# Two VectorE operations of the first division moved one period later, in a fused routing-attention and act-serf kernel

## The chip, the cores and the metric

The kernel runs on one core of a Trainium2 chip. The metric is the device time of one execution, in microseconds; the time of a kernel is the median over its runs. The engines named below are TensorE (PE in the profile, its weight loads PEld), VectorE (DVE), ScalarE (ACT), GpSimd (POOL) and SyncE (SP), which here only issues DMAs (SPq is its queue).

## What is computed

Attention for 4 batches, 8 heads, 768 positions and 64 values per head, where a query sees only the keys that fall to the same of 16 centroids; its output is the input of a two-layer network with a gate between the layers.

```python
q_assign = np.argmax(np.einsum('bhsd,hcd->bhsc', q_n, c_n), axis=-1)
k_assign = np.argmax(np.einsum('bhsd,hcd->bhsc', k_n, c_n), axis=-1)
mask = q_assign[:, :, :, None] == k_assign[:, :, None, :]
scores = scale * np.matmul(q, k.transpose(0, 1, 3, 2))
scores = np.where(mask, scores, -1000000000.0)
scores = scores - np.max(scores, axis=-1, keepdims=True)
attn = np.exp(scores)
attn = attn / (np.sum(attn, axis=-1, keepdims=True) + 1e-09)
attn_out = np.matmul(attn, v)
...
h = x @ w_in                                  # x: 3072 x 512, w_in: 512 x 2048
sp = np.maximum(h, 0.0) + np.log1p(np.exp(-np.abs(h)))
g = h * erf(sp)
out = g @ w_out                               # w_out: 2048 x 512
```

## The kernel before

The 32 heads are worked on in 16 pairs, numbered from 0. A pair has 12 units: a unit is one half of the queries (384 of 768) against one tile of 128 keys, six units to a half. The attention runs as a sequence of periods, `period(p, i)` with i from 0 to 5, and each period does the matmuls of two units, so six periods make a pair and three make a half. The second layer of the kernel, the network, follows and takes the rest of the span.

Every engine call goes through a wrapper that keeps the program's order on its engine, so what is written first in `period` runs first on that engine. No planner moves anything there; the queues are in the order in which the Python code makes them, and semaphores between engines follow from which tile is written and read.

A period has these parts, in the order of the code:

- A step of the maxima, `step_ahead(p, 2 * i)`. For a tile of 128 queries of a later half or pair, low-precision products go into the PSUM tile `wide` (rows `wide<-kv,qv`, then `wide<-km,qm`, which add the routing mask), and VectorE reduces them to the negated maxima, `nmx<-wide`. There is one `wide`, so the next step's matmuls wait for this reduction.
- A call of `next(part[0], None)`, which advances a division by one piece (below).
- The products of query and key of the first unit, `sc<-qT,kT`, then `mask(3)`, then those of the second unit. Where the table `FIRST_MASKS` (for the first pair) or `MASKS` (for the others) has an entry, `mask` issues a matmul `turned<-hotT,pick` or `turned<-aside,pick` that writes 384 columns of a PSUM tile `turned`, and ScalarE copies these to the mask rows `qm` or `km`. For the first pair the table has an entry at i = 5, place 3: the second half of `qm` of the second pair, in `turned[0]`.
- A second step of the maxima, `step_ahead(p, 2 * i + 1, True)`, in three pieces, with the mask matmuls of the scores, `sc<-qm,km`, between its matmuls. These need the row of shifts of their half (the negated row maxima), which is row 0 and row 64 of `qm`.
- The second call of `next(part[0], None)`, which is the one that the change touches (L1466).
- ScalarE's exponentials, `pr<-sc`, the sums over units on GpSimd, `more_out<-more_out,pr`, and the products with the values, `turned<-pr,in_v`, of the two units before.
- At i = 0 and i = 3 the start of the division of the half just finished.

A step that ends a half also calls `into_rows`: VectorE reduces the maxima to `least`, transposes them to `least_rows`, and SyncE issues four DMAs `qm<-least_rows` that put the row of shifts in place. In the first pair, i = 5, the first step (the tenth that is counted from the pair's start) does this for the first half of the second pair; `scores` of the second pair's first unit, in the period after, reads that row.

`divide(u)` is a generator. Its first piece issues the matmuls `turned<-more_out,minus` and two ScalarE operations `inv`. The second piece is VectorE's `den<-turned,inv` and the first `turned<-turned,inv` (128x192). The third is the second `turned<-turned,inv` and then `more_out<-den,turned` (128x384), which reads the numerators out of the PSUM tile `turned` and leaves the quotients in SBUF. The fourth issues four DMAs `x_dram<-more_out`. The first division (the first half of the first pair) begins at i = 3 and has its numerators in `turned[0]`. Its second and third piece come at i = 4, one at each call of `next(part[0], None)`, and its fourth at the first call in i = 5.

Of the kernel before, what the change touches and what calls it, by code (L numbers as in the profile page):

```python
# [28 lines left out]
HJ = NJ // 2  # L29
# [110 lines left out]
def kernel(  # L140
# [182 lines left out]
    def sign(n):  # L323
        hi, _, upper = steps[n]
        ae.activation(out=upper, in_=hi, func=ACT.Prelu, scale=2.0**-25, alpha=2.0**90)
# [51 lines left out]
    def transposes(p, which="qk"):  # L377

        if p >= NPAIR:
            return  # L380
        st = pairs[p]
        for nm in which:
            st[nm + "T"] = rows[p % 3][nm]
            ve.transpose(out=st[nm + "T"], in_=st.pop(nm).rearrange("p n t -> p (n t)"))
        if "k" in which:
            st.update(lows[p % 2])
            if p > 1:
                load_qk(p + 1)
# [10 lines left out]
    def similarities(p, groups=range(4), lo=0, hi=HW):  # L399

        if p >= NPAIR:
            return
        st = pairs[p]
        st["psim"] = turned[1][:, 0:HW]
        for g in groups:
            te.matmul(
                st["psim"][2 * C * g : 2 * C * (g + 1), lo:hi], lhsT=ccT[:, p % HP],
                rhs=st["qk"[g // 2] + "T"][:, g % 2 * HW + lo : g % 2 * HW + hi],
                start=True, stop=True,
            )  # L410

    def choose(p, spare=None, aside=False):

        if p >= NPAIR:
            return
        st = pairs[p]
        n = HW // C
        sims = routep.tile([P, HW], F32, name="sims")
        ve.transpose(out=sims, in_=st.pop("psim"))
        yield  # L420
        sim = sims.rearrange("p (g c) -> p g c", c=C)
        mx = (wide[:, 0] if spare is None else spare)[:, 512 - n :]
        ve.reduce_max(out=mx, in_=sim, axis=AX.X)
        yield
        hot = routep.tile([P, HW], BF16, name="hot")
        ve.tensor_tensor(
            out=hot.rearrange("p (g c) -> p g c", c=C), in0=sim,
            in1=mx.unsqueeze(2).to_broadcast([P, n, C]), op=ALU.is_equal,
        )
        yield  # L430
        if aside:
            st["aside"] = routep.tile([P, HW], BF16, name="aside")
            ve.transpose(out=st["aside"][D + Q :], in_=hot[D : D + Q])
            yield
        st["hotT"] = routep.tile([P, HW], BF16, name="hotT")
        ve.transpose(out=st["hotT"], in_=hot)
# [5 lines left out]
    def masks(p, nm, half, bank, narrow=False, copied_by=ae):  # L442

        if p >= NPAIR:
            return lambda: None
        st = pairs[p]
        cols = slice(half * HW, (half + 1) * HW)
        r, hot = slice(0, D) if nm == "q" else slice(D, P), st["hotT"]
        picked = pick[r, half]
        if narrow:  # L450
            r = slice(r.start + Q, r.stop)
            picked = pick[r, 1]
            hot = hot if half else st["aside"]
        won = bank[:, 0:HW]
        te.matmul(won, lhsT=picked, rhs=hot[r], start=True, stop=True)
        if nm == "q":
            return lambda: ae.activation(out=st["qm"][:, cols], in_=won, func=ACT.Relu)
        if copied_by is ve:
            return lambda: ve.tensor_scalar(
                out=st["km"][:, cols], in0=won, scalar1=BIG, scalar2=nbig, op0=ALU.mult, op1=ALU.add  # L460
            )
        return lambda: ae.activation(
            out=st["km"][:, cols], in_=won, func=ACT.Identity, bias=nbig, scale=BIG
        )
# [82 lines left out]
    def turn(p, h):  # L547

        st = pairs[p]
        pn = turned[h][:, 0:HW].rearrange("p (t n) -> p t n", t=HJ)  # L550
        for t in range(HJ):
            for e in range(2):
                cols = slice(e * D, e * D + Q)
                te.matmul(pn[cols, t], lhsT=lowest[h][:, t, cols], rhs=identb, start=True, stop=True)
        for e in range(2):
            r = slice(e * D, e * D + 1)
            ae.copy(out=st["qm"][r, h * HW : (h + 1) * HW], in_=pn[r].rearrange("p t n -> p (t n)"))
        st["shift", h] = True
# [832 lines left out]
    def run(work):  # L1391
        for _ in work:
            pass
# [19 lines left out]
    part = [iter(())]  # L1413

    def period(p, i):
        u = 2 * NJ * p + 2 * i
        n1, n2 = 2 * p - 1, 2 * p
        early = lambda n: 0 <= n < N_EARLY

        def mask(place):  # L1420
            which = (MASKS if p else FIRST_MASKS).get((i, place))
            if which:
                return masks(p + 1, *which, turned[0 if i in (0, 5) else 1], place == 2)
            return lambda: None

        if u > 0:
            for which in turns if i in (0, 3) else ():
                turn(*which)
                turns.remove(which)
            if i == 3 and not p:  # L1430
                transposes(2, "k")
            if i == 3 and p:
                similarities(p + 2)
                routing[0] = choose(p + 2, turned[0], True)
            step_ahead(p, 2 * i)
            if i == 3 and p:
                next(routing[0], None)
            if i == 2:
                transposes(p + 2, "k" if p else "q")
        mask(0)()  # L1440
        if i == 0 and early(n1 - 1):
            sign(n1 - 1)
        elif i == 3 and early(n1):
            sign(n1)
        if i == 4:
            next(routing[0], None)
        next(part[0], None)
        if i == 0 and p:
            run(routing[0])
            transposes(p + 2, "q")  # L1450
        if u == 2:
            next(routing[0])
            next(routing[0])
        products(u)
        mask(3)()
        products(u + 1)
        mask(1)()
        second = step_ahead(p, 2 * i + 1, True) if u > 0 else iter(())
        next(second, None)
        if u == 0:  # L1460
            step_ahead(0, 1)
        rows = D if u == 0 or u + NJ + 2 >= len(units) else Q
        scores(u, rows)
        next(second, None)
        next(second, None)
        next(part[0], None)  # L1466
        if i == 5:
            next(routing[0], None)
        scores(u + 1, rows)
        later = mask(2)  # L1470
        if i == 3 and not p:
            similarities(p + 2)
            routing[0] = choose(p + 2, turned[0], True)
        if i == 0:
            later()
            curve(u)
        else:
            curve(u)
            later()
        curve(u + 1)  # L1480
        if u == 0:
            similarities(1)
            routing[0] = choose(1, turned[1])
            next(routing[0])
            vectors(1, "q")
            vectors(1, "k")
        if i == 0 and early(n1 - 1):
            bounded(n1 - 1)
            shifted(n1 - 1)
        elif i == 1 and early(n1):  # L1490
            size_and_rest(n1)
        elif i == 5 and early(n2):
            rest(n2)
        for _ in range(FORMS.get(p, {}).get(i, 0)):
            x_forms.pop(0)() if x_forms else forms.pop(0)[0]()
        if i == 3:
            if not p:
                next(routing[0], None)
            if early(n1):
                bounded(n1)  # L1500
                shifted(n1)
        elif i == 1:
            load(p + 1, "v", v, vp)
            if p == 0:
                run(routing[0])
        elif i == 4:
            vectors(p + 2, "k")
            vectors(p + 2, "q")
        if u > 0:
            if i == 1 and early(n1 - 1):  # L1510
                summed(n1 - 1)
            elif i == 4 and early(n1):
                summed(n1)
            if i in POOL_FORMS.get(p, ()) and forms:
                forms.pop(0)[1]()
            for w in (u - 2, u - 1):
                accumulate(w)
            for w in (u - 2, u - 1):
                attend(w)
            if i == 3:  # L1520
                next(routing[0], None)
            if i % HJ == 0 and u - 1 != LATE or u - 3 == LATE:
                part[0] = divide(u - 1 - u % NJ)
                next(part[0])
        if i == 3 and early(n2):
            size(n2)
# [74 lines left out]
    u = len(units)  # L1601
# [101 lines left out]
```

## Time and profile before

| | us |
|---|---|
| median of 3 runs | 945.91 |
| lowest and highest of them | 945.71 and 1938.44 |
| the profiled execution | 945.83 |
| its span, first to last instruction | 944.1 |
| TensorE busy in the span | 938.0 |
| VectorE busy in the span | 784.3 |
| period i = 4 of the first pair, by its first `wide` matmul | from 33.45 |
| period i = 5 of the first pair | from 37.40 |
| period i = 0 of the second pair | from 41.49 |

The profiled execution took 1.73 us more than its span; that is what lies before the first and after the last instruction. In a timeline each row has the start and the duration in microseconds, the engine, the line, the operation, what it writes and reads, and how many instructions are merged in it; a bracket at the end gives the idle time before it and what ended that. All instructions carry L131, since the wrapper of the engines issues them, so they are told apart by their tiles. In the chain of waits each row is a stretch of the path that ended last.

### The profile page before, as it was taken

The page shows a single profiled execution, that of the slowest core. Times are in us where ns is not written, and L with a number is a line of the kernel's source. Part 1 is how long each engine was busy: PE and PEld are TensorE (multiplying, and loading weights), DVE is VectorE, ACT ScalarE, POOL GpSimd, SP SyncE. Part 2 cuts the span into 40 slices and gives each one's busy share as a digit, 9 for nine tenths or more (in the row PEclk, how much of TensorE's full clock was granted, in tenths as well). Part 3 has the DMA queues.
Part 4 walks back from the last instruction along what each step waited for, and adds up shares of the span by engine and source line. Part 5 has one row for each costly group of instructions (what it writes and reads, how often), then busy time and mean ns, then how long its engine had stood idle before and what let it go on. Part 6 is the DMA issues. An engine that isn't in the chain of part 4 may idle for free.

```text
span 944.1 us, 22367 instructions
## 1 busy us (share of the span) xinstructions
PE 938.0 (99%) x8775; PEld 708.9 (75%) x8775; DVE 784.3 (83%) x1416; ACT 546.6 (58%) x809; POOL 506.4 (54%) x365
## 2 busy tenths in 40 slices
PE   8999999999999999999999999999999999999998
PEld 4555555555555555688888889998999899989987
DVE  8888888888888887879886688689868977897887
ACT  4777777777777776476413553663257236525541
POOL 2688888888888888999119111450063016103600
PEclk9999999999999999999999999999999999999999
DMA  9345545554443621133875257353453436343433
GB/s 215 79 112 113 113 113 114 113 114 112 113 112 68 156 56 38 24 128 127 219 249 219 83 125 221 106 175 118 151 176 128 136 120 202 118 150 123 157 112 111
DMA packets 176352, 123.17 MB, mean 130 GB/s; under 512 B 132600, under 2 KB 143352, under 8 KB 176248
## 3 DMA queue, kind: packets, MB, share of 16 engines
q1 hardware_dynamic: 171880, 116.34, 43.2%
q0 software_dynamic: 1872, 4.98, 2.9%
q8 instruction: 69, 1.13, 0.5%
q10 hardware_dynamic: 2496, 0.43, 0.2%
q14 instruction: 35, 0.29, 0.1%
HBM read 91.78 MB, written 23.33 MB: 122 GB/s over the span
## 4 chain that ended last, share of the span: by engine, by line
PE 98%; DVE 1%; SPq 0%; DMA 0%; issue 0%; DVEq 0%
PE bank L131 43%; PE turned L131 32%; PE sc L131 17%; PE wide L131 6%; DVE nmx L131 1%; SPq L131 0%; DMA qm<-least_rows 0%; DVE sims L131 0%; DVE hotT L131 0%; DVE wide L131 0%; DVE hot L131 0%; DVE qm L131 0%; DVE qT L131 0%; DVE osb L131 0%; DVEq L1698 0%
## 5 line engine op out<-in xcount | busy, mean ns | idle before, releaser
L131 POOL TENSOR_TENSOR more_out<-more_out,pr 128x768 f32<-128x768 f32 x128 | 217.1, 1696 | 15.4 <-ACT pr L131 5.4
L131 DVE TENSOR_REDUCE nmx<-wide 128x2 f32<-128x512 f32 (+4 forms) x189 | 179.4, 950 | 45.6 <-PE wide L131 44.5
L131 ACT ACTIVATE pr<-sc 128x768 f32<-128x768 f32 x192 | 148.4, 810 | 80.4 <-PE wide L131 73.8
L131 PE MATMUL turned<-pr,in_v 128*32 128x193 f32 x3072 | 145.2, 330 | 0.0
L131 POOL TENSOR_TENSOR g<-g 128x512 f32<-128x512 f32 x36 | 47.1, 1308 | 180.8 <-DVE g L131 178.9
L131 PEld LDWEIGHTS turned<-pr,in_v 128*32 128x32 f32 x3072 | 90.2, 109 | 51.0 <-issue 27.0
L131 DVE TENSOR_TENSOR g<-g 128x512 f32<-128x512 f32 x132 | 90.8, 688 | 23.2 <-PE bank L131 12.2
L131 PE MATMUL sc<-qT,kT 64*128 64x384 f32 x528 | 98.7, 485 | 0.0
L131 DVE TENSOR_TENSOR g<-bank,g 128x256 f32<-128x256 f32 (+1 forms) x128 | 64.6, 531 | 18.2 <-PE bank L131 9.5
L131 PE MATMUL bank<-g_more,g 128*128 128x256 f32 (+1 forms) x328 | 75.7, 374 | 0.0
L131 PE MATMUL bank<-x_own,w_in 128*128 128x128 f32 (+1 forms) x440 | 74.0, 310 | 0.0
L131 ACT ACTIVATE a_s<-g 128x1024 f32<-128x1024 f32 x38 | 39.6, 1055 | 57.5 <-POOL g L131 44.7
L131 POOL TENSOR_TENSOR more_out<-pr,pr 128x768 f32<-128x768 f32 x32 | 59.6, 1861 | 14.9 <-ACT pr L131 14.9
L131 PEld LDWEIGHTS bank<-g_more,g 128*128 128x128 f32 x328 | 61.2, 190 | 8.1
L131 PEld LDWEIGHTS bank<-x_own,w_in 128*128 128x128 f32 x440 | 63.2, 191 | 4.4 <-issue 0.6
L131 DVE TENSOR_TENSOR g<-a_s,g 128x512 f32<-128x512 f32 x76 | 66.2, 892 | 0.4 <-ACT a_s L131 0.4
L131 PE MATMUL wide<-kv,qv 64*128 64x512 bf16 (+4 forms) x380 | 64.4, 326 | 0.5 <-DVE nmx L131 0.5
L131 PE MATMUL bank<-w_out,g 128*128 128x256 f32 x280 | 64.5, 379 | 0.0
L131 PE MATMUL wide<-km,qm 32*128 32x512 bf16 (+5 forms) x380 | 62.0, 325 | 0.0
L131 ACT ACT_TABLE_LOAD x40 | 51.3, 1283 | 17.9 <-DVE g L131 17.3
L131 PEld LDWEIGHTS <-qv 64*128 64x128 bf16 x386 | 23.0, 93 | 51.4 <-issue 37.1
L131 PEld LDWEIGHTS sc<-qT,kT 64*128 64x128 f32 x528 | 46.3, 187 | 18.6 <-issue 1.3
(245 smaller groups left out, 1992.6 us busy)
## 6 DMA issues: line engine op xcount, KB each, us to landing
g_more<-b_dram SPq DMA_DIRECT2D x52, 512.0 KB
g_more<-w_dram SPq DMA_DIRECT2D x84, 256.0 KB
x_own<-in_moe_w_in_dram SPq DMA_DIRECT2D x13, 512.0 KB
in_v<-in_v_dram SPq DMA_DIRECT2D x32, 192.0 KB
x_dram<-more_out SPq DMA_DIRECT2D x128, 48.0 KB
x_own<-x_dram SPq DMA_DIRECT2D x6, 1024.0 KB
in_k<-in_k_dram SPq DMA_DIRECT2D x59, 96.0 KB
in_q<-in_q_dram SPq DMA_DIRECT2D x58, 96.0 KB
```

The costliest lines, as they stand in the source:

```text
L131: ins = getattr(self.engine, name)(*args, **kw)
```

## The change

One call of `next(part[0], None)` is left out in one period, that of u = 8, which is the first pair at i = 4 (HJ is 3, and u is 12 p + 2 i).

```diff
@@ -1463,7 +1463,8 @@
         scores(u, rows)
         next(second, None)
         next(second, None)
-        next(part[0], None)
+        if u != 2 * (HJ + 1):
+            next(part[0], None)
         if i == 5:
             next(routing[0], None)
         scores(u + 1, rows)
```

The generator of the first division is thereby one piece behind at the end of i = 4. Its third piece comes at the first call in i = 5, which stands behind the first step of that period and its `into_rows`, and its fourth at the second call of i = 5. On VectorE the order was

```
nmx x2 | turned<-turned,inv | more_out<-den,turned | nmx | least | memset nmx | least_rows | nmx
```

and is now

```
nmx x2 | nmx | least | memset nmx | least_rows | turned<-turned,inv | more_out<-den,turned | nmx
```

No instruction is added or taken away, on this engine or another. On SyncE the four `x_dram` DMAs follow the four `qm<-least_rows` DMAs in both kernels. TensorE, ScalarE and GpSimd have the same instructions in the same order.

## The prediction

> **What bounds the kernel now.** I read the page's totals first, then the chain of waits from the period after the change to the end, then the same chain around the change.
>
> ```profile
> span 944.1 us, 22367 instructions
> PE 938.0 (99%) x8775; PEld 708.9 (75%) x8775; DVE 784.3 (83%) x1416; ACT 546.6 (58%) x809; POOL 506.4 (54%) x365
> by line: PE bank L131 45.2%; PE turned L131 32.2%; PE sc L131 16.6%; PE wide L131 5.7%; DVE osb L131 0.0%; DVEq L1698 0.0%; issue 0.0%
> ```
>
> The third line is the chain restricted to 44 us and later, that is, to everything behind the place of the change. Its four TensorE entries add up to 99.7%. TensorE's queue is the path from there to the end, so a delay of that queue, or a gain, near 40 us should reach the end in full. Now the chain at the change:
>
> ```profile
> 36.07 1.28 DVE L131 TENSOR_REDUCE nmx<-wide 128x2 f32<-128x352 f32 x2
> 37.26 0.42 DVE L131 SCALAR_TENSOR_TENSOR turned<-turned,inv 128x192 f32<-128x192 f32 x1
> 37.72 0.56 DVE L131 SCALAR_TENSOR_TENSOR more_out<-den,turned 128x384 f32<-128x384 f32 x1
> 38.19 1.05 DVE L131 TENSOR_REDUCE nmx<-wide 128x2 f32<-128x864 f32 x1
> 39.35 0.18 DVE L131 TENSOR_REDUCE least<-nmx 128x6 bf16<-128x18 f32 x1
> 39.58 0.27 DVE L131 STREAM_TRANSPOSE least_rows<-least 128x96 bf16<-128x96 bf16 x1
> 40.06 1.23 DVE L131 TENSOR_REDUCE nmx<-wide 128x2 f32<-128x1024 f32 x1 [0.20 <-PE wide L131]
> ```
> ```profile
> 40.00 0.75 SPq L131
> ...
> 41.93 1.49 DMA qm<-least_rows
> 43.42 0.14 issue
> 43.56 0.34 PE sc L131 x2
> ```
> ```profile
> 37.40 0.36 PE L131 MATMUL wide<-kv,qv 64*128 64x432 bf16 x2
> 37.58 0.36 PE L131 MATMUL wide<-km,qm 64*128 64x432 bf16 x2
> 37.76 0.82 PE L131 MATMUL sc<-qT,kT 64*128 64x384 f32 x4
> 38.40 0.32 PE L131 MATMUL turned<-hotT,pick 64*128 64x384 bf16 x1
> 38.42 0.95 PE L131 MATMUL sc<-qT,kT 64*128 64x384 f32 x4
> 39.30 0.39 PE L131 MATMUL wide<-kv,qv 64*128 64x512 bf16 x2
> 39.62 0.33 PE L131 MATMUL sc<-qm,km 32*128 32x384 bf16 x2
> 39.63 0.39 PE L131 MATMUL wide<-km,qm 32*128 32x512 bf16 x2
> 41.49 0.28 PE L131 MATMUL wide<-kv,qv 64*128 64x256 bf16 x2
> 43.56 0.34 PE L131 MATMUL sc<-qm,km 32*128 32x384 bf16 x2 [0.17 <-DMA qm<-least_rows]
> ```
>
> The first fence is VectorE: the two operations to be moved (37.26 and 37.72) and, right behind them, the row step that ends in `least_rows`. The second is the one stretch behind 20 us where the chain leaves TensorE for a transfer: the row of shifts, issued by SyncE from 40.00, lands at 43.42, and the second pair's first scores begin at 43.56 because of it. The third is TensorE over the same time. Two things matter in it: the scores at 43.56 wait, and the mask's matmul `turned<-hotT,pick` at 38.40 stands ahead of everything else of that period.
>
> **The moved operations, and what they hold up.** In the old order they take VectorE from 37.26 to 38.19, 0.93 us ahead of the row step. That step's matmuls end at 37.58 + 0.36 = 37.94, and a reduction starts 0.04 behind the matmuls it waits for (39.63 + 0.39 = 40.02 against 40.06). With the two gone from the front it starts at 37.98: the row gains 0.21 us and not 0.93, because TensorE is then the late one.
>
> The rest of the row step keeps its spacing: `least` 1.16 behind the reduction (38.19 to 39.35), `least_rows` 0.23 behind that (39.35 to 39.58), so 39.14 and 39.37. The memset between them has no room of its own in the old order and gets none here. What follows such a transpose without a wait starts 0.20 later, as in the second pair:
>
> ```profile
> 51.10 0.28 DVE L131 STREAM_TRANSPOSE least_rows<-least 128x96 bf16<-128x96 bf16 x1
> 51.30 0.95 DVE L131 STREAM_TRANSPOSE kT<-in_k 128x768 f32<-128x768 f32 x1
> ```
>
> The first moved operation therefore starts at 39.57, the second 0.46 later (37.26 to 37.72), at 40.03, and it ends 0.56 later, at 40.59. In the old order that end was 37.72 + 0.56 = 38.28.
>
> This end releases the mask's matmul. The matmul writes 384 columns of `turned[0]`; the second moved operation reads the first division's numerators from the same columns (386 of them), so the matmul may not start before it has ended. In the old order it began at 38.40, 0.12 behind that end, with the first unit's products just through, so the wait cost nothing visible. Now it begins about 0.05 behind 40.59 (the `wide` matmuls at 37.40 begin 0.05 behind the reductions that hold them, 36.07 + 1.28 = 37.35): at 40.64. **TensorE stands for 40.64 - 38.40 = 2.24 us.** Queued behind this matmul on TensorE are the second unit's products, the second step of the maxima, both units' mask scores and the products with the values; ScalarE's exponentials wait for the scores, GpSimd's sums for the exponentials, VectorE's next reduction for `wide`. Nobody has other work to offer TensorE there.
>
> What the stall consists of is thus VectorE's own chain: 1.05 + 0.18 + 0.27 of the row step with its gaps, which the mask never had to wait for, and the 0.93 of the moved pair, less the 0.21. I take the stall as between 2.1 and 2.4 us: the gaps between VectorE operations in these rows scatter by about 0.1, and so does the release.
>
> **What the stall pays back.** Two waits that TensorE has now lie behind it.
>
> ```profile
> 45.82 0.28 PE L131 MATMUL wide<-kv,qv 64*128 64x256 bf16 x2
> 47.65 0.34 PE L131 MATMUL sc<-qm,km 32*128 32x384 bf16 x2
> 50.41 0.96 PE L131 MATMUL sc<-qT,kT 64*128 64x384 f32 x4
> 51.47 0.34 PE L131 MATMUL sc<-qm,km 32*128 32x384 bf16 x2
> ```
>
> First, the transfer. From the first `wide` matmul of a period to its first mask scores takes 47.65 - 45.82 = 1.83 us where nothing is waited for, and 43.56 - 41.49 = 2.07 in the period that waits for the row. The wait is worth 0.24 us. In the new order the row lands 0.21 earlier, at 43.21, while TensorE arrives two microseconds later, so it is gone altogether. Second, the wait for `wide`. From the second unit's products to the mask scores takes 51.47 - 50.41 = 1.06 in a period with a mask at the same place, and 39.62 - 38.42 = 1.20 here, where the second step's matmuls at 39.30 follow the row step's reduction (38.19 + 1.05 = 39.24). By then the reduction is long done, so 0.14 goes. Together 0.38 us come back.
>
> The other queues: the `x_dram` DMAs stood behind the row's four DMAs on SyncE already.
>
> ```profile
> 42.48 1.82 SPq L131 DMA_DIRECT2D x_dram<-more_out  x4
> 38.76 0.50 ACT L131 ACTIVATE qm<-turned 128x384 bf16<-128x384 f32 x1
> 41.01 3.45 POOL L131 TENSOR_TENSOR more_out<-more_out,pr 128x768 f32<-128x768 f32 x2 [0.72 <-ACT pr L131]
> 45.38 0.51 PE L131 MATMUL turned<-more_out,minus 128*32 128x192 f32 x8
> ```
>
> Their source is ready at 40.59, before SyncE gets to them at 42.48 - 0.21 = 42.27; this costs nothing, and the cover, 1.7 us, is ample. ScalarE's copy of the mask begins 0.36 behind its matmul (38.40 to 38.76) and lasts 0.50; shifted it ends at 41.50. The `wide<-km,qm` matmuls that read it stand at 39.63 and come at 39.63 + 2.24 - 0.14 = 41.73, so 0.23 us of cover is left; if ScalarE were later than that, the rest would be added. GpSimd's sum ends at 41.01 + 3.45 = 44.46 and its reader on TensorE starts at 45.38: 0.92 us of slack, of which the vanished transfer wait eats 0.24. All of these move with TensorE, and none becomes the late one.
>
> **Sum.** 2.24 - 0.14 - 0.24 = +1.86 us on the profiled execution: 945.83 + 1.86 = 947.69. The median of the runs shown, 945.91, lies 0.08 higher, which is less than the spread of the runs that agree (945.71 to 945.91), so I state 947.7.
>
> **Rivals.**
>
> *The mask does not wait* (faster). The place is the matmul at 38.40. If it, or the products behind it, can run while VectorE is still busy with the row step, only the gains are left: the 0.14, and 0.21 of the 0.24, as the row lands 0.21 earlier. That is 945.83 - 0.35 = 945.48. It decides at 38.40: if the matmul still starts there, this holds. For it speaks that no row shows this matmul waiting; against it that its output columns and the ones that the division reads are the same, and that in the old order it started only 0.12 us behind the division's end. [...] Chance 0.05.
>
> *The stall is absorbed later* (no change, 945.83). This needs a place behind 44 us where TensorE waits for something that does not move with it. The restricted chain above leaves 0.3% for all else, so I see none. Chance 0.03.
>
> *ScalarE becomes late.* If the copy of the mask comes later than its 0.23 us of cover allows, at most its length of 0.50 is added: 948.2. Chance 0.08.
>
> *The stall costs TensorE its clock.*
>
> ```profile
> 0.00:4.00 4.00, 2.87 (x14) 1.87 (x15) 1.91 (x21) 1.69 (x3) 2.97 (x21) 1.00 0.67 107
> 40.00:44.00 4.00, 3.83 (x57) 1.98 (x53) 3.84 (x5) 3.44 (x4) 3.20 (x3) 1.00 0.08 19
> ```
>
> In these rows by stretches (bounds, length, busy time of PE, PEld, DVE, ACT and POOL, then the granted clock) the clock is 1.00, with 1.13 us of TensorE idle in the first and 0.17 in the second. No row has a gap of 2.24 us. If the clock were halved for one period after it, the work between 41.49 and 45.82 would take 4.33 us more: 947.69 + 4.33 = 952.0. [...] Chance 0.04.
>
> **How the numbers follow.** The forecast has 0.80; the chances of the five add up to 1. Its own bounds are 945.83 + 2.1 - 0.38 = 947.55 and 945.83 + 2.4 = 948.23, where nothing is paid back. With twice the runs' spread of 0.20 on either side this is 947.15 to 948.63, and I give 947.1 to 948.6. It takes in the late ScalarE and leaves out the mask that does not wait, the absorbed stall and the lost clock, 0.12. Two per cent, about what a measurement of this kernel can tell from no change, is 18.9 us; every case here stays far within it, so I give 0.98 to that and 0.01 to each side for what I have not thought of.
>
> **What would show it.** On VectorE, `least_rows` about 0.2 us earlier and `more_out<-den,turned` ending near 40.6. On TensorE, the mask's matmul near 40.6 with an idle time of about two microseconds before it that names VectorE, and scores in the next period without a wait for `qm<-least_rows`. In the chain, a stretch of VectorE between 38 and 40.6 in place of the transfer. The prediction is wrong if the mask's matmul still stands near 38.4, if the distance of TensorE's rows to those of the kernel before shrinks again after 50 us, or if the granted clock falls under 1.00.

## The result and the profile after

| | before | after |
|---|---|---|
| median, us | 945.85 (8 runs) | 949.20 (8 runs) |
| the profiled execution, us | 945.83 | 949.37 |
| its span, us | 944.1 | 947.7 |
| mean granted TensorE clock in it | 1.000 | 0.998 |

The ratio of the times is 1.0031, with a 95% interval from 1.0021 to 1.0040 (the two medians alone would give 1.0035). One of the eight runs of the kernel before took 1938.44 us and is left out of the ratio. The changed kernel is slower by a third of a per cent, and the 949.20 lies above the range of 947.1 to 948.6. The eight runs of the changed kernel fall on two levels: three at 947.49, 947.60 and 947.60 with a mean clock of 1.000, and five from 949.14 to 949.44 with a clock of 0.998. The profile is of one on the upper level.

The first fence is VectorE and the head of TensorE's waits, from the timeline and the list of waits of the changed kernel (a wait row has the total, the number of waits and the longest).

```profile
37.97 1.06 DVE L131 TENSOR_REDUCE nmx<-wide 128x2 f32<-128x864 f32 x1 [0.63 <-PE wide L131]
39.37 0.27 DVE L131 STREAM_TRANSPOSE least_rows<-least 128x96 bf16<-128x96 bf16 x1
39.57 0.40 DVE L131 SCALAR_TENSOR_TENSOR turned<-turned,inv 128x192 f32<-128x192 f32 x1
40.00 0.55 DVE L131 SCALAR_TENSOR_TENSOR more_out<-den,turned 128x384 f32<-128x384 f32 x1
PE turned L131 <- DVE more_out L131: 2.0, 1, 2.0
```

The row step starts 0.22 us earlier (37.97 for 38.19), waits for TensorE as foretold, and the moved pair ends at 40.55. The new wait of TensorE names `more_out`. Now TensorE's own timeline:

```profile
40.61 0.47 PE L131 MATMUL turned<-hotT,pick 64*128 64x384 bf16 x1 [2.03 <-DVE more_out L131]
40.62 1.74 PE L131 MATMUL sc<-qT,kT 64*128 64x384 f32 x4
42.06 0.73 PE L131 MATMUL wide<-kv,qv 64*128 64x512 bf16 x2
42.72 0.50 PE L131 MATMUL sc<-qm,km 32*128 32x384 bf16 x2
43.47 1.75 PE L131 MATMUL turned<-pr,in_v 128*32 128x193 f32 x32
45.15 0.28 PE L131 MATMUL wide<-kv,qv 64*128 64x256 bf16 x2
46.99 0.34 PE L131 MATMUL sc<-qm,km 32*128 32x384 bf16 x2
```

The mask's matmul starts at 40.61, with 2.03 us of idle time before it. The durations behind it have changed too. The four products behind it take 1.74, where the same four took 0.95 in the kernel before; the `wide` pair takes 0.73 in place of 0.39. From the mask's matmul to the next period's first `wide` matmul are 45.15 - 40.61 = 4.54 us, in the kernel before 41.49 - 38.40 = 3.09. From there the old pace is back: 46.99 - 45.15 = 1.84, with no wait for the row of shifts, which was 2.07 with it. The stretches of 0.4 us below (bounds, length, busy time of PE, PEld, DVE, ACT and POOL, and then the granted clock) tell why:

```profile
38.40:38.80 0.40, 0.18 (x2) 0.00 (x0) 0.40 (x1) 0.40 (x1) 0.32 (x2) 1.00 0.00 0
...
40.00:40.40 0.40, 0.00 (x0) 0.00 (x0) 0.40 (x1) 0.00 (x0) 0.30 (x1) 1.00 0.00 0
40.40:40.80 0.40, 0.19 (x2) 0.19 (x3) 0.16 (x1) 0.00 (x0) 0.00 (x0) 0.74 0.00 0
40.80:41.20 0.40, 0.40 (x3) 0.40 (x4) 0.00 (x0) 0.08 (x1) 0.00 (x0) 0.50 0.01 1
...
43.60:44.00 0.40, 0.40 (x8) 0.26 (x11) 0.40 (x1) 0.40 (x1) 0.00 (x0) 0.50 0.51 123
44.00:44.40 0.40, 0.40 (x17) 0.24 (x10) 0.40 (x1) 0.40 (x2) 0.12 (x1) 0.99 0.48 117
```

The granted clock is 0.50 in every stretch from 40.80 to 44.00. A mean of 0.74 in the stretch before means that it fell 0.21 us ahead of 40.80, at 40.59; a mean of 0.99 in the last one, that it rose at 44.01. It was halved for 3.42 us, and half of that, 1.71 us, is lost if all of TensorE's work runs at half its pace. The two levels differ by 949.3 - 947.6 = 1.7.

### The profile page after: what moved, and what is told of

Same layout as the page of the kernel before. It is cut to its first block, busy times and chain, and to the rows that moved or that the text cites. A ratio compares the mean times of both kernels' runs of the same rounds, so it can differ in the third digit from the quotient of the medians.

```text
span 947.7 us, 22368 instructions
## 1 busy us (share of the span) xinstructions
PE 939.6 (99%) x8775; PEld 709.3 (75%) x8775; DVE 783.3 (83%) x1416; ACT 546.5 (58%) x809; POOL 506.7 (53%) x365
## 4 chain that ended last, share of the span: by engine, by line
PE 98%; DVE 1%; issue 0%; DVEq 0%
PE bank L131 43%; PE turned L131 32%; PE sc L131 17%; PE wide L131 6%; DVE nmx L131 1%; DVE sims L131 0%; DVE hotT L131 0%; DVE wide L131 0%; DVE more_out L131 0%; DVE hot L131 0%; DVE qm L131 0%; DVE qT L131 0%; DVE turned L131 0%; DVE osb L131 0%; DVEq L1699 0%
```

## The experiments

The two theories before them: A, that the stall costs 1.7 us by itself, and that the idle time before the mask's matmul halves the clock in some runs, which costs another 1.7; B, that the second level has another cause and the clock only goes with it.

**The idle time filled with useless matmuls.** In the changed kernel, between the products of the first unit and the mask:

```diff
         products(u)
+        if u == 10:
+            filler = ps_s.tile([P, 2, 512], F32, name="sc", tag="s")
+            of_filler.append(filler)
+            for _ in range(FILL):
+                te.matmul(filler[:, 0, 0:P], lhsT=identb, rhs=identb, start=True, stop=True)
         mask(3)()
```

`FILL` is 18, a constant in a new line ahead of the wrapper, so that the rows of this kernel carry L132. In a line that is not shown, the second unit's products take `filler` as their tile and overwrite it.

> The changed kernel, with 18 matmuls 128x128 of no use put on TensorE between the first unit's products and the mask's matmul, into a PSUM tile that the second unit's products overwrite. They fill the time in which TensorE stood idle (2.03 us in the profile after) and should fit into it. Theory A (the stall costs 1.75 us, and in some runs TensorE's clock is halved after it because of the idle time, which costs another 1.7): the stall stays, the clock does not fall, all runs at 947.4 to 947.8 with a mean clock of 1.000. Theory B (the second level of the runs has another cause in the changed order, and the clock only marks it): still two levels, some runs near 949.3.

Measured: 947.70 against 945.82, ratio 1.0020 (1.0011 to 1.0029). All 11 runs lie from 947.43 to 947.98, three of them above the 947.8 that was expected, with a clock of 1.000. From TensorE's timeline of this kernel:

```profile
38.25 1.18 PE L132 MATMUL sc<-identb 128*128 128x128 bf16 x18
40.34 0.32 PE L132 MATMUL turned<-hotT,pick 64*128 64x384 bf16 x1 [0.91 <-DVE more_out L132]
40.35 0.95 PE L132 MATMUL sc<-qT,kT 64*128 64x384 f32 x4
41.45 0.34 PE L132 MATMUL sc<-qm,km 32*128 32x384 bf16 x2
43.33 0.28 PE L132 MATMUL wide<-kv,qv 64*128 64x256 bf16 x2
45.16 0.34 PE L132 MATMUL sc<-qm,km 32*128 32x384 bf16 x2
```

The mask still waits for the same VectorE operation and as long (2.85 us from the first unit's products to the mask here, from 37.49, and in the changed kernel, from 37.76), but only 0.91 us of it is idle, and the products behind it take 0.95 again. The upper level is gone, and the stall's own price is left. This separates the two parts: B is refuted. The useless matmuls change what TensorE did last as well as the length of its idle time; the experiment with three of them, below, separates these.

**The mask's matmul out of the way.** In the changed kernel the table's entry moves from i = 5 to i = 3, where it writes `turned[1]`:

```diff
-FIRST_MASKS = {(2, 0): ("q", 0), (2, 3): ("k", 0), (2, 2): ("k", 1), (5, 3): ("q", 1)}
+FIRST_MASKS = {(2, 0): ("q", 0), (2, 3): ("k", 0), (2, 2): ("k", 1), (3, 1): ("q", 1)}
```

> The changed kernel, with the mask's matmul of i = 5 moved to i = 3, where it writes the other PSUM tile and has nothing to do with the first division. The new order on VectorE stays. Theory A: the whole loss is this matmul's wait, so nothing of it is left: 945.7 to 945.9, clock 1.000, no TensorE wait for more_out<-den,turned. Rival (the two operations cost time where they now stand, because VectorE gets behind): 946.5 or more.

Measured: 945.90 against 945.82, ratio 1.0002 (0.9993 to 1.0010). The whole loss hung on this one matmul. Two rows of this kernel show that the new order is not free, though, only paid for elsewhere:

```profile
40.49 1.22 DVE L131 TENSOR_REDUCE nmx<-wide 128x2 f32<-128x1024 f32 x1
41.76 0.28 PE L131 MATMUL wide<-kv,qv 64*128 64x256 bf16 x2 [0.39 <-DVE nmx L131]
```

With TensorE no longer standing, VectorE's next reduction is the late one (behind the moved pair, without idle time), and `wide` comes free 0.39 us late.

**The same move in the old order.** The table's entry as above, in the kernel before.

> The kernel before, with only the mask's matmul moved from i = 5 to i = 3; the order on VectorE is the old one. It tells what that move is worth by itself. If the new order costs nothing once the mask is out of the way and gains nothing either (the run with both was 945.90), this is 945.8 to 945.95. If the new order did bring the row's 0.2 us there and something else ate it, this run shows a wait for qm<-least_rows near 0.2 us and no wait of wide for nmx at 41.76.

Measured: 945.99 against 945.79, ratio 1.0002 (0.9993 to 1.0011), a little above what was expected. The wait for the row of shifts is there (0.16 us of idle time before the scores at 43.69), that of `wide` for `nmx` is not. So the new order did buy off the row's wait, for one of about the same size. By the first `wide` matmuls of the periods, i = 5 takes 4.35 us with the new order (37.41 to 41.76) and 4.10 with the old (37.53 to 41.63), and the period after it 4.10 (to 45.86) and 4.32 (to 45.95).

**One more reduction ahead of the moved pair.** The idle time becomes longer:

```diff
+        if u == 10:
+            idle_for = small.tile([P, 1], F32, name="idle_for")
+            ve.reduce_max(out=idle_for, in_=rows_of_first["q"], axis=AX.X)
         next(part[0], None)
```

> The changed kernel, with one more VectorE reduction (128x768, near 0.95 us, of no use) ahead of the two moved operations, so that TensorE stands idle for about 3.0 us in place of 2.0. [...] Theory B: the same mixture as before, some runs near 948.5 and some near 950.2.

Measured: five runs, at 948.22 (clock 1.000), 949.69, 949.69, 949.77 (0.997 to 0.998) and 951.17 (0.996), against 945.82, ratio 1.0041 (1.0028 to 1.0054). TensorE stood idle for 2.88 us. Four of five fell (here and below, a run has fallen when its mean clock is 0.998 or less). My levels were 0.3 to 0.5 too high: the idle time grew by 0.85 us and not by 0.95, and the levels lie 1.5 apart and not 1.7; the rest is open. The run at 951.17 lost about twice as much clock as the others. The mask's matmul and the clock in the profile of the run at 949.77:

```profile
41.23 0.32 PE L131 MATMUL turned<-hotT,pick 64*128 64x384 bf16 x1 [2.88 <-DVE more_out L131]
```
```profile
41.20:41.60 0.40, 0.36 (x3) 0.35 (x4) 0.00 (x0) 0.01 (x1) 0.00 (x0) 1.00 0.01 1
...
42.00:42.40 0.40, 0.40 (x4) 0.00 (x0) 0.00 (x0) 0.08 (x1) 0.00 (x0) 0.75 0.01 1
42.40:42.80 0.40, 0.40 (x8) 0.13 (x6) 0.00 (x0) 0.00 (x0) 0.00 (x0) 0.50 0.01 1
...
45.20:45.60 0.40, 0.40 (x12) 0.12 (x4) 0.00 (x0) 0.40 (x1) 0.40 (x1) 0.50 0.00 0
45.60:46.00 0.40, 0.40 (x12) 0.20 (x6) 0.00 (x0) 0.40 (x1) 0.32 (x2) 0.98 0.00 0
```

Here TensorE is at work again from 41.23 on at the full clock, and the clock falls only at 42.20, 0.97 us later, and rises at 45.62: once more 3.42 us. In the profile of the changed kernel it fell at 40.59, 0.02 us ahead of the mask's matmul. The idle time began at 41.23 - 2.88 = 38.35 here and at 37.76 + 0.82 = 38.58 there, so the fall comes 3.85 and 2.01 us behind its beginning. It is thus at no fixed distance from the idle time's end or its beginning; what places it, these two profiles do not show.

**The pair between the reduction and `least`.** A shorter idle time:

```diff
             else:
+                if (p, h) == (1, 0):
+                    next(division[0])
                 into_rows(p, h, nmx, HJ - 1 if in_parts else 0, HJ)
```

In a line that is not shown, `division` is made another name of `part`, the list with the generator.

> The two moved operations stand behind the row step's reduction, but ahead of least and least_rows. TensorE stands idle for about 1.4 us in place of 2.0 and loses 1.57 against the old order, of which 0.14 and 0.24 come back. [...] Theory B: two levels, 947.0 and 948.7, in a mixture like that of the changed kernel.

Measured: 946.88 against 945.82, ratio 1.0010 (1.0001 to 1.0019). Idle for 1.43 us, all 11 runs between 946.67 and 947.01, none fell.

**One of the two moved.** In the kernel before, the first division gets one more stop, so that only `more_out<-den,turned` comes behind the row step:

```diff
-            if k == 0:
+            if k == 0 or u == NJ - 1:
                 yield
```

> Only the second of the two operations, more_out<-den,turned, is moved behind the row step; the first keeps its old place, and the mask stays at i = 5. TensorE then stands idle for about 1.6 us. The stall is 0.43 shorter than in the changed kernel: 947.1 (946.95 to 947.3). [...] Rival (any long gap can cool it, the chance growing smoothly with the gap): some runs near 948.7.

Measured: 947.17 against 945.79, ratio 1.0015 (1.0006 to 1.0024). Idle for 1.56 us, none of 11 runs fell.

**Three useless matmuls.** The first experiment with `FILL = 3`:

> The changed kernel with 3 matmuls of no use in the gap in place of 18, which leaves TensorE idle for about 1.85 us. [...] Rival (what the 18 matmuls changed was not the length of the gap but what TensorE had just done): one level at 947.6.

Measured: seven runs, median 947.78 against 945.79, ratio 1.0027 (1.0016 to 1.0038). Idle for 1.75 us. That is 0.10 less than expected. Two runs fell (949.32 and 949.86, clock 0.998), so that useless matmuls alone do not keep the clock. Four lie from 947.45 to 947.78; one at 948.32, with a clock of 1.000, fits neither level and I can't explain it.

**Two more reductions.** The experiment with a longer idle time, with its reduction twice:

> [...]

Measured: six runs, median 951.67 against 945.86, ratio 1.0063 (1.0050 to 1.0075). Idle for 3.86 us. All six fell, three with a clock of 0.998 (950.94 to 951.16) and three with 0.996 (952.17 to 952.46). Half of the runs thus lost about twice as much clock, and their times lie 1.0 to 1.5 us above the others. The profile of the run at 951.16, in stretches of 1 us:

```profile
40.00:41.00 1.00, 0.00 (x0) 0.00 (x0) 0.96 (x2) 0.00 (x0) 0.23 (x1) 1.00 0.00 0
...
43.00:44.00 1.00, 1.00 (x11) 0.12 (x6) 0.00 (x0) 0.22 (x1) 0.00 (x0) 0.77 0.41 98
...
46.00:47.00 1.00, 1.00 (x18) 0.27 (x12) 0.00 (x0) 0.97 (x2) 0.92 (x2) 0.52 0.00 0
```

TensorE is idle from 38.52 to 42.38. The clock falls at 43.54, 1.16 us after TensorE is at work again, and rises at 46.96: 3.42 us once more.

**The changed kernel again.**

> The changed kernel itself, to see the two levels on the same chip as the longer gap. [...] Rival (the share of cooled runs belongs to the chip or the day): another share, near none or near all.

Measured: all five runs fell, from 949.19 to 949.60, against 945.86. With the eight above that is 10 of 13. Five of five is also what the rival gives, so that it is not excluded, and the share is not pinned down. The profile of the run at 949.40 has the same program with its fall at another place: the mask's matmul starts at 40.61 behind 2.03 us of idle time, as in the profile after, but the clock falls at 40.82 and rises at 44.24 (means of 0.91 from 40 to 41 and of 0.88 from 44 to 45), 0.23 us later than there, again for 3.42 us.

Together, by the idle time that the profile shows before the mask's matmul:

| idle, us | kernel | runs | fell |
|---|---|---|---|
| 0.91 | 18 useless matmuls | 11 | 0 |
| 1.43 | pair ahead of `least` | 11 | 0 |
| 1.56 | one of the two moved | 11 | 0 |
| 1.75 | 3 useless matmuls | 7 | 2 |
| 2.03 | the changed kernel, twice | 13 | 10 |
| 2.88 | one reduction more | 5 | 4 |
| 3.86 | two reductions more | 6 | 6 |

None of the 33 runs with an idle time of 1.56 us or less fell, and 22 of the 31 with 1.75 us or more did; no kernel lies between. The counts allow a chance that grows steeply between 1.56 and 2.03 us. In the four profiles of fallen runs the clock fell 2.01, 2.24, 3.85 and 5.02 us behind the beginning of the idle time, each time for 3.42 us. What decides whether a run falls, and when, no run shows.

**A version from this: one moved, and the mask at i = 3.**

> As the run with one operation moved, and the mask's matmul at i = 3. VectorE stands idle between 37.35 and 37.98 in the run with the mask moved, and the first operation fits there, so that neither the row nor the reduction behind the moved operation comes late: the row lands 0.2 earlier and nothing waits for VectorE. 945.65 (945.55 to 945.75), which would beat both kernels by a little. Rival (VectorE is the bound of this stretch, and what it gains in one place it gives back in the next): 945.8 to 945.95, with a wait of wide for nmx.

Measured: 945.62 against 945.79, ratio 0.9999 (0.9990 to 1.0008). From the timelines of this kernel:

```profile
37.16 0.42 DVE L131 SCALAR_TENSOR_TENSOR turned<-turned,inv 128x192 f32<-128x192 f32 x1
37.87 1.06 DVE L131 TENSOR_REDUCE nmx<-wide 128x2 f32<-128x864 f32 x1 [0.29 <-PE wide L131]
41.19 0.28 PE L131 MATMUL wide<-kv,qv 64*128 64x256 bf16 x2
43.24 0.34 PE L131 MATMUL sc<-qm,km 32*128 32x384 bf16 x2 [0.16 <-DMA qm<-least_rows]
```

The first operation fits into VectorE's idle time, the `wide` matmul at 41.19 waits for nothing, and the row's transfer is the late one again, but earlier. From the first `wide` matmul of i = 5 the two periods take 8.22 us (37.29 to 45.51), in the kernel before 8.42 (37.40 to 45.82). Its median is 0.17 us under that of the kernel before, as expected, but the interval holds 1: it is not shown to be faster.

## Why the prediction was wrong

*The chain and the path.* Right. TensorE's queue carries the delay to the end: in the profile after, the matmuls `turned<-more_out,minus` of the second division come 3.42 us late (48.80 for 45.38) and those of the thirty-first 3.43 (408.12 for 404.69), and the span is 3.6 longer.

*The row gains 0.21 us, not 0.93.* Right: 38.19 became 37.97, and the reduction waits for `wide`.

*The mask's matmul waits until 40.64, and TensorE stands 2.24 us.* Right: 40.61, 2.21 after its old place. The experiment with the mask at i = 3 shows that the loss hangs on this matmul. That the mask does not wait is refuted by its new place, and that the stall is absorbed by the times. ScalarE did not become late: TensorE's list of waits has none for the copy of this mask, in the changed kernel, where the copy ends at 41.12 + 0.49 = 41.61 and its reader starts at 42.73, or in the one with the idle time filled.

*0.38 us come back.* Right within 0.04. In the kernel with the idle time filled, whose clock stays full, the time from the second unit's products to the mask scores is 41.45 - 40.35 = 1.10 (1.20 before), so 0.10 came back where the sum had 0.14; from the next period's first `wide` matmul to its scores it is 45.16 - 43.33 = 1.83 (2.07 before), the whole 0.24. That makes 2.21 - 0.34 = 1.87, and the median of that kernel lies 1.88 over that of the kernel before (947.70 and 945.82), where the sum had 1.86. The three runs of the changed kernel with a full clock average 1.71 over 945.85, within the scatter of the 11 runs (947.43 to 947.98) but too few to say more. At a full clock the sum was thus right in its parts and not by luck.

*The clock stays.* This is the step that failed. The prediction put the rival at 0.04, and the range left it out; a granted clock under 1.00 is one of the prediction's own signs of being wrong. That the clock stays through 2.24 us of idle time was the author's estimate: in the kernel before TensorE has no wait of that length, the longest is 1.1 us. 10 of 13 runs of the changed kernel, with 2.03 us, had a mean clock of 0.998, and the median is such a run; of those with 1.75 us 2 of 7 fell, with 1.56 none of 11. The price was off as well. The half speed and the whole period in the rival's 4.33 us are shown by no run of the kernel before; in the four profiles of fallen runs the clock was halved, but for 3.42 us. What that cost, from the mask's matmul to the next period's first `wide` matmul: 45.15 - 40.61 = 4.54 us in the profile after, against 43.33 - 40.34 = 2.99 with the idle time filled, so 1.55, and 1.58 or 1.59 in the other three profiles; the two levels lie 1.7 apart in the changed kernel and 1.5 in the one with one reduction more.

*The chances.* Both kernels lie far within two per cent of each other, as given.

## What to carry to other kernels

Before an operation is moved behind another on a busy engine, look for whoever waits for its end, and at what stands behind that waiter in its queue: here two operations of half a microsecond each were off the path, and a small matmul that reused their PSUM tile put them onto it. A wait of TensorE cost its own length here, less what came back behind it (1.88 us for a stall of 2.21 where the clock stayed full). With 1.75 to 3.86 us of idle time 22 of 31 runs also lost clock, which cost about 1.6 us more, and in four of them about twice as much clock was lost; with 0.91 to 1.56 us none of 33 did. So price an idle time of TensorE as long as those with a chance of that, and look at the single runs' clocks and not at the median alone. Where the wait can't be taken away, useless matmuls that shorten the idle time can keep the clock, as in all 11 runs with 18 of them (0.91 us).

## What was unexpected in the hardware

The clock does not follow the idle time at a fixed distance. In the four profiles of fallen runs it fell 2.01 to 5.02 us behind the beginning of the idle time, in two of them 0.97 and 1.16 us after TensorE was at work again, and it was at 0.50 for 3.42 us each time. The same program has two times: three runs of the changed kernel took 947.49 to 947.60 us with a clock of 1.000, and ten took 949.14 to 949.60 with 0.998. What makes the difference between them was not shown; the two profiles of that program, both of fallen runs, have the fall 0.23 us apart, at 40.59 and 40.82. The shortest idle time with a fallen run is 1.75 us, the longest of a kernel without one 1.56. Why one run with 2.88 us of idle time and three with 3.86 lost about twice as much clock (0.996) was not tried, and none of these four has a profile.
